# A transformer block in one core: combinations of half blocks, output pops and low halves given out in another order in the feed-forward stage

## The chip, the cores and the metric

The kernel runs on one core of a Trainium2 chip. Times are device microseconds (us) of one execution; the kernel before took 1749.36 us (median of three runs, 1748.49 to 1750.36). The engines are called PE (TensorE, matmuls), DVE (VectorE), ACT (ScalarE), POOL (GpSimd) and SP (SyncE, which issues nearly all DMAs). Each works through its own queue strictly in order, and waits where an operand or a buffer is not ready.

## What is computed

```
mod = (silu(c) @ w_mod) in six parts: sa, ca, ga, sb, cb, gb
h = layernorm(x) * (1 + ca) + sa
x = x + ga * attention(h)                      # 32 heads, 512 keys, wq, wo, cached k and v
h = layernorm(x) * (1 + cb) + sb
x = x + gb * ((gelu(h @ w_gate) * (h @ w_up)) @ w_down)
```

x has 2048 rows of 512 columns, and the feed-forward width F is 1792. All is given and returned in float32.

## The kernel before

**Precision by halves.** Every operand of a large matmul is kept as two float16 tiles, a high half (the rounded value) and a low half (the rest). A product is three matmuls (`mm3`, line 90): low times high, high times high, high times low. The third one is the one that needs the low half of the moving operand. A high half is made by ACT with a copy, a low half by DVE or POOL with a subtraction that reads the high half, so a low half always comes after ACT.

**Seven products for eight.** The projections are computed by a Strassen-like scheme (the Winograd form): a product of 2 x 2 blocks takes seven block products instead of eight, of sums and differences of blocks. `PROD` names the seven products; the feed-forward stage takes them in the order `ORDER = (1, 2, 6, 7, 5, 4, 3)`. Products accumulate in three PSUM banks `fa`, `fb`, `fc`. After products 1, 6 and 7 ACT copies the bank `fa` out (`keep`, line 887) before the next product goes on in it; the results 11, 22, 21 and 12 are made by DVE additions to those copies (line 1272).

**The rows.** The 2048 rows are two halves of 1024. For the second half ("second rows", generation 3) the moving operands of the seven products are the blocks b11, b21, b22 and the combinations t1 to t4. `combos` makes them, in two pairs p=0 and p=1 (two of the four 128-column tiles each): four loads of 256 KB from device memory into raw buffers (`cb`, a pool of five), then seven high halves on ACT (line 374), four differences on POOL (line 576) and seven low halves on POOL (line 378). Each piece has an offset, 0 to 8, which says in what order the pieces come.

**The feed-forward stage** is written out without a scheduler: what Python calls is what the queues get, in that order. It runs over quarters q = 0 to 27. Quarter q belongs to the pair of F tiles n = q // 2 (14 pairs, seven for each half of the rows); even quarters compute the gate (gelu on ACT), odd ones the up product, multiplied on DVE with the gate (line 1288). A quarter has seven places k = 0 to 6, one per product. `step(s, fn)` puts a piece of work at quarter s // 7, place s % 7. At each place these come in order: the product with what follows on it, the pieces of `step`, the work that was put off until now (`put_off(n, fn)` with `tick`), then possibly one pop.

**Activations.** In the odd quarter of pair n the four results are multiplied and split into high half (ACT, line 1298) and low half (line 1302). For n % 7 < 5 the pair is "turned": its down projection uses the seven products too, so behind result 12, the last of the quarter, POOL makes four sums of the results (`sums_of`, line 1314), ACT their high halves and POOL their low halves t1 to t4 (line 1302 on POOL), spread over the next quarter by `put_off`. The other pairs (n = 5, 6, 12, 13) make no sums.

**The down projection** of a turned pair is `yt_tasks(n)`: 14 products in two runs of seven (p = 0, 1), in banks `ya`, `yb`, `yc`, handed out two at a time ("a pop") by `y_next()`. The 14 tasks of pair n enter the list at place k=2 of quarter 2n+2. A pop comes at the places k = 1, 2, 5 and 6 of each quarter. After each y product DVE adds the bank to the result (`yt_add`, lines 1679 and 1682), and the next y product on that bank must wait for it. The first pop has products 1 and 2, the second 6 and 5: product 6 takes t2 and product 5 takes t1. With the last turned pair of a half (n = 4, 11), ACT also makes eight copies of the results (`yu`, line 1698) which SP transposes with DMAs, and POOL adds them to the rows.

**Queue of SP.** Weight sets for quarter q + 1 are fetched from device memory at places k = 2, 3, 4 of quarter q; the loads of the combinations stand in the same queue.

**Where the combinations stand before.** Pair p=0 has its loads at step 59 and its offsets at steps 61, 63, 65 ... 77, pair p=1 at step 73 and 75, 77 ... 91 (`q = 61 + 14 * p`, `step(q + 2 * off, fn)`, lines 1649 to 1654). The results 12 of n=3 and n=4, with which the sums begin, come at steps 55 and 69.

Of the kernel before, what the change touches and what calls it, by code (L numbers as in the profile page):

```python
# [64 lines left out]
def block_kernel(ctx: ExitStack, tc: tile.TileContext, x, kT, v, wq, wo, wg, wu, wd, cT, wc, wm, out):  # L65
    nc = tc.nc
# [7 lines left out]
    def tmp(name):  # L74
        return pool.tile([P, 512], F32, tag="e", name=name, bufs=NE)
# [4 lines left out]
    def pair(tag, name, bufs):  # L80
        return pool.tile([P, 2, 512], F16, tag=tag, name=name, bufs=bufs)
# [96 lines left out]
    def col(name, i=0):  # L178
        return ST[name][:, i:i + 1]
# [113 lines left out]
    def turned(n):  # L293

        return n % NP < NP - NROW
# [160 lines left out]
    def put_off(n, fn):  # L456

        if n == 0:
            return fn()
        waits_.append([n, fn])  # L460
# [219 lines left out]
    def k_items(pr):  # L680
        g = pr // 2
        st, load = reader(kT[g])
        m = {}

        def stat():
            m["m"] = little("lm", 4, dtype=BF16)
            sumsq(m["m"][:, 0:1], st["r"])

        def spread(go=True, ps=None):
            return k_spread(g, m["m"], go, ps)  # L690

        def parts(first=False):
            KV[0, pr, 0] = t = get_k()
            if first:
                return split_post(t, st["r"], col("ksc", pr))
            times(st["r"], col("ksc", pr))
            halves(t, st["r"])

        return (load, stat, spread, parts) + ((m,) if pr == 0 else ())

    def v_items(g):
        st, load = reader(v[g])
        m = {}

        def stat():
            m["m"] = little("lm", 4, dtype=BF16)
            sumsq(m["m"][:, 0:1], st["r"])

        def spread():
            w = little("lw", 1, 2)  # L710
            norm2(col("vmax", g), m["m"], 1, 1.0)
            pool_ts(w, col("vmax", g), 1.0 / TOP14)
            if g:
                y_scale(g)
            then(lambda: nc.vector.reciprocal(col("vsc", g), w), 3 if g > 1 else 2)

        def parts():
            KV[0, g, 1] = get_v()
            times(st["r"], col("vsc", g))
            halves(KV[0, g, 1], st["r"])  # L720

        return load, stat, spread, parts
# [162 lines left out]
    def keep(st, k, t):  # L885
        st[k] = t
        nc.scalar.activation(t, st["a"], AF.Copy)  # L887

    def kept(k):
        return pool.tile([P, QB], F32, tag=k, name=k, bufs=1)  # L890
# [117 lines left out]
    def low(t):  # L1008
        p16 = E[t]["p16"]
        nc.vector.scalar_tensor_tensor(p16[:, 1, :], E[t]["e"], E[t]["r"], p16[:, 0, :], op0=ALU.mult, op1=ALU.subtract)  # L1010
        u, i = divmod(t, 4)
        if i == 0:
            pT[u] = pool.tile([P, QT, 2 * KT, P], F16, tag="pt", name="pt", bufs=NPT)
        nc.sync.dma_start_transpose(pT[u][:, i], p16.rearrange("p a b -> p (a b)"))
        E.pop(t)
# [196 lines left out]
    for g in range(NG):  # L1212
# [24 lines left out]
        else:  # L1237
            if g > 0:
                if pr % 2 == 0:
                    load, stat, spread_, parts = k_items(pr)  # L1240
                    sched(t0 - (22 if g > 2 else 20), (load, [stat]))
                    at(("w", t0 - (19 if g > 2 else 17)), spread_)
                load, stat, spread_, parts = k_items(pr)
                sched(t0 - (7 if g > 2 else 8 if g > 1 else 6), (load, [parts if g != 2 else lambda parts=parts: soon(parts(True))]))
                at(t0 - (3 if g > 2 else 1 if g > 1 else 2), lambda pr=pr: store(("k", pr), KV[0, pr, 0]))
                if pr % 2 == 0:
                    load, stat, spread_, parts = v_items(qd)
# [7 lines left out]
    NQ = 4 * NP  # L1255
# [7 lines left out]
    def f_scale(q):  # L1263
        return (q // 2) % NP * 2 + q % 2

    def f_items(q, hold=None):
        n, m = divmod(q, 2)
        st = {}
        done = set()

        def add(k, src):
            nc.vector.tensor_tensor(st[k], st[k], st[src], op=ALU.add)

        def gelu(key, src):

            def apply():
                dst = tmp("fg") if key == "21" else src
                nc.scalar.activation(dst, src, AF.Gelu_apprx_tanh, scale=col("finv", f_scale(q)))
                G[n, key] = dst

            return (apply,)

        def result(key, src):
            if m == 0:
                put_off(2 if key == "11" else 0, gelu(key, src)[0])
            else:
                g = G[n, key]
                nc.vector.scalar_tensor_tensor(g, g, col("gsc", n % NP), src, op0=ALU.mult, op1=ALU.mult)  # L1288
                if not turned(n):
                    parts(key, G.pop((n, key)))  # L1290
                elif key != "12":
                    parts(key, g)
                else:
                    sums_of()

        def high_of(key, g):
            t = A[n, key] = pair("ot", "at", NOT)
            nc.scalar.activation(t[:, 0, :], g, AF.Copy)  # L1298

        def low_of(key, g, eng):  # L1300
            t = A[n, key]
            eng.tensor_tensor(t[:, 1, :], g, t[:, 0, :], op=ALU.subtract)  # L1302

        def parts(key, g):
            high_of(key, g)
            if key == "21":
                st["low"] = lambda: low_of(key, g, nc.vector)
            else:
                put_off(3 if key == "11" else 2, lambda: low_of(key, g, nc.vector))

        def sums_of():
            g = {k: G.pop((n, k)) for k in ("11", "12", "21", "22")}
            for o, a, b in (("11", "12", "11"), ("12", "22", "12"), ("22", "22", "11"), ("21", "21", "22")):
                nc.gpsimd.tensor_tensor(g[o], g[a], g[b], op=ALU.subtract)  # L1314
            late = 0 if n else 2
            for key, o, high, low in (("t1", "11", 2, 5), ("t3", "12", 3, 6), ("t2", "22", 4, 5), ("t4", "21", 5, 6)):
                put_off(high + (late if high < 5 else late // 2), lambda key=key, o=o: high_of(key, g[o]))
                put_off(low + late // 2, lambda key=key, o=o: low_of(key, g[o], nc.gpsimd))

        def out_(key, src):  # L1320
            if not hold:
                result(key, src)
            else:
                hold.append(gelu(key, src))

        def place(k):
            if m == 0:
                return pool.tile([P, QB], F32, tag="k", name="fg", bufs=2) if k == "u2" and n else tmp("fg")
            return pool.tile([P, QB], F32, tag="p16", name="fu", bufs=NP16) if k == "s1" else kept(k)

        def after(k):
            done.add(k)
            if k in (1, 6, 7):
                name = {1: "s1", 6: "u2", 7: "u3"}[k]
                keep(st, name, place(name))
            if k == 2:
                add("s1", "b")
                out_("11", st["s1"])
            elif k == 4:
                out_("21", st["a"])  # L1340
            elif k == 3:
                if "low" in st:
                    st["low"]()
                add("u2", "c")
                out_("12", st["u2"])
            if k in (5, 7) and {5, 7} <= done:
                add("u3", "c")
                out_("22", st["u3"])

        tags = {"a": ("s", "fa", 2) if q else ("qa", "fa", 1), "b": ("acc", "fb", NACC), "c": ("acc", "fc", NACC)}  # L1350
        return with_posts(("f", q), 2 + q // (2 * NP), banks(st, tags), after)

    def f_spread_at(q):
# [284 lines left out]
    def step(q, fn):  # L1638
        f_at(q // 7, q % 7, fn)

    for i, q in enumerate((16, 19, 22, 26, 30, 33, 36, 40)):
        load, norm, split, turn = ln_turned(i)
# [3 lines left out]
        step(q + 4, turn)  # L1646
    for q, (qb, dt) in zip((37, 41, 44, 47, 50, 51, 54, 55), ((0, 0), (0, 2), (0, 1), (0, 3), (1, 0), (1, 2), (1, 1), (1, 3))):
        step(q, lambda qb=qb, dt=dt: turned_out(qb, dt))
    for p in range(2):
        q = 61 + 14 * p  # L1650
        for load, steps in combos(3, p, nc.gpsimd):
            step(q - 2, load)
            for off, fn in steps:
                step(q + 2 * off, fn)

    def whole(ti):
        if ti in halfway and ti in joined:
# [100 lines left out]
    for q in range(NQ):  # L1758
        n, m = divmod(q, 2)
        its = items(NG + q) if q < 2 else f_items(q)  # L1760
        for k, pk in enumerate(ORDER):
            if (q, pk) not in f_done:
                all_of(its[pk])
            run(("f", q, k))
            tick()
            if n and k == 2 and m == 0 and turned(n - 1):
                nexty += yt_tasks(n - 1)
            if k in ((1, 2, 5, 6) if q < NQ - 1 else (2, 5)):
                y_next()
        if m == 1 and not turned(n):  # L1770
            for qi, (a, b) in enumerate((("11", "21"), ("12", "22"))):
                for i in range(QT):
                    nexty.append(y_tasks((2 * (n // NP) + qi) * QT + i, [lambda n=n, a=a: A[n, a], lambda n=n, b=b: A[n, b]],
                                         [("f", n, 0), ("f", n, 1)], col("dysc", n % NP), f_final))
# [40 lines left out]
```

## Time and profile before

| what | value |
|---|---|
| median of three runs | 1749.36 us (1748.49 to 1750.36) |
| the profiled execution, whole | 1748.16 us |
| its span on the core | 1745.9 us |
| PE, DVE, ACT, POOL busy | 98%, 82%, 71%, 61% |
| mean granted PE clock | 0.998 |
| feed-forward stage | from about 1355 us to the end |

How to read it: the span is the profiled execution from its first to its last instruction, and the time of a run has some 2.3 us around that. A row of the timeline gives start, duration, engine, line, operation, tile written and tiles read, and the number of equal instructions merged; in brackets the idle time of the engine before it and whose result ended that. A row of the windows gives, after the length, the busy time and the number of instructions of PE, PE's weight loads, DVE, ACT and POOL, then the granted PE clock, the busy share of the DMA engines and GB/s. Matmuls overlap, so the duration of a row with six of them is longer than the distance to the next row.

### The profile page before, as it was taken

Reading aid. Unit: us, or ns where it says so; the run is one execution under the profiler, and the core shown is the slowest. Engines: PE = TensorE matmul, PEld = TensorE weight load, DVE = VectorE, ACT = ScalarE, POOL = GpSimd, SP = SyncE. Lnnn points to the kernel's source line nnn. Section 1 sums busy time; section 2 is a strip of 40 time slices with the busy share of each in tenths; the row PEclk is TensorE's granted clock in tenths of the full one; section 3 lists DMA queues with packets and bytes.
Section 4 is the critical chain, followed back from the end, with each engine's and each line's share of the span. In section 5 each row is a group of like instructions: output and inputs, shape, how many; then the busy total and the mean of one; then the engine's idle time right before and its main releaser. Section 6 shows DMA issues by size and latency. Waiting matters only on the chain.

```text
span 1745.9 us, 26253 instructions
## 1 busy us (share of the span) xinstructions
PE 1716.3 (98%) x8022; PEld 787.6 (45%) x8022; DVE 1423.4 (82%) x2462; ACT 1243.0 (71%) x2797; POOL 1056.9 (61%) x1274
## 2 busy tenths in 40 slices
PE   7999999999999999999999999999999999999998
PEld 5444444444444444444444444444444444344444
DVE  7898898888889899888888888888986787566666
ACT  6988788888879777887777777787774455433442
POOL 4889778776788884655575675654521335643424
PEclk9999999999999999999999999999999999999999
DMA  7999999999999999999999999999986564733353
GB/s 232 220 205 212 211 216 207 222 208 217 215 219 230 208 204 185 212 208 232 202 215 231 213 215 211 205 228 213 196 184 145 153 175 151 191 126 113 95 154 104
DMA packets 690636, 339.82 MB, mean 195 GB/s; under 512 B 578880, under 2 KB 601408, under 8 KB 690496
## 3 DMA queue, kind: packets, MB, share of 16 engines
q1 hardware_dynamic: 690208, 337.63, 85.9%
q8 instruction: 63, 1.03, 0.2%
q14 instruction: 77, 0.63, 0.1%
q10 hardware_dynamic: 288, 0.52, 0.1%
HBM read 135.66 MB, written 61.87 MB: 113 GB/s over the span
## 4 chain that ended last, share of the span: by engine, by line
PE 85%; DVE 5%; ACT 4%; POOL 2%; DMA 2%; issue 1%; SPq 0%; POOLq 0%; DVEq 0%; ACTq 0%
PE py L90 19%; PE po L90 17%; PE ps L90 17%; PE qa L90 8%; PE fa L90 7%; PE qc L90 4%; PE fc L90 4%; PE ya L90 2%; PE qb L90 2%; PE fb L90 2%; DMA pt<-p 1%; PE yc L90 1%; ACT ee L993 1%; ACT p L1005 1%; PE pq L90 1%
## 5 line engine op out<-in xcount | busy, mean ns | idle before, releaser
L993 ACT ACTIVATE ee<-ps,nm 128x512 f32<-128x512 f32 x512 | 350.1, 684 | 189.8 <-DVE nm L984 187.7
L1010 DVE SCALAR_TENSOR_TENSOR p<-ee,rr,p 128x512 f16<-128x512 f32 x512 | 459.9, 898 | 4.5 <-ACT p L1005 4.1
L984 DVE TENSOR_REDUCE nm<-ps 128x1 f32<-128x512 f32 x512 | 350.6, 685 | 106.9 <-PE ps L90 103.7
L90 PE MATMUL ps<-k,qt 128*128 128x512 f16 x1536 | 414.9, 379 | 5.2 <-ACT ee L993 4.1
L1005 ACT ACTIVATE p<-ee,rr 128x512 f16<-128x512 f32 x512 | 364.5, 712 | 20.9 <-DMA pt<-p 10.5
L90 PE MATMUL po<-pt,v 128*128 128x512 f16 x1536 | 373.0, 379 | 2.6 <-DMA pt<-p 2.6
L90 PE MATMUL py<-wo,ot 128*128 128x512 f16 x1536 | 371.5, 379 | 0.0
L90 PEld LDWEIGHTS <-w 128*128 128x128 f16 x2184 | 213.7, 98 | 261.8 <-issue 5.8
L90 PEld LDWEIGHTS <-v 128*128 128x128 f16 x1536 | 149.9, 98 | 184.9 <-DMA pt<-p 2.4
L90 PEld LDWEIGHTS <-ot 128*128 128x128 f16 x1536 | 150.2, 98 | 181.6 <-DVE ot L742 0.5
L90 PEld LDWEIGHTS <-qt 128*128 128x128 f16 x1536 | 145.9, 98 | 176.6 <-issue 4.4
L1314 POOL TENSOR_TENSOR fg<-fg 128x512 f32<-128x512 f32 x40 | 52.6, 1315 | 163.9 <-DVE fg L1288 161.5
L742 DVE SCALAR_TENSOR_TENSOR ot<-po,ot 128x512 f16<-128x512 f32 x128 | 87.8, 686 | 36.7 <-ACT ot L741 36.3
L1298 ACT ACTIVATE at<-fg 128x512 f16<-128x512 f32 x86 | 53.9, 627 | 88.8 <-DVE fg L1288 75.0
L993 ACT ACTIVATION_READ_ACCUMULATOR ee<-ps,nm 128x1 f32 x512 | 100.0, 195 | 0.0
L954 DVE SCALAR_TENSOR_TENSOR acc<-py,ysc,acc 128x512 f32<-128x512 f32 x128 | 94.7, 740 | 5.3 <-PE py L90 5.3
L235 POOL TENSOR_TENSOR lw<-lw,half__86 128x1 f32<-128x1 f32 x37 | 23.3, 631 | 105.2 <-DVE lw L185 105.1
L90 PE MATMUL qa<-t,w 128*128 128x512 f16 x348 | 84.9, 379 | 0.0
L90 PE MATMUL fa<-t,w 128*128 128x512 f16 x336 | 81.6, 379 | 1.3 <-ACT fg L887 0.8
L397 POOL TENSOR_TENSOR rs<-rs,nhalf 128x1 f32<-128x1 f32 x32 | 18.7, 585 | 102.0 <-DVE rs L391 99.1
L741 ACT ACTIVATE ot<-po 128x512 f16<-128x512 f32 x128 | 73.9, 577 | 5.0 <-PE po L90 5.0
L90 PE MATMUL ya<-at,wo 128*128 128x512 f16 x240 | 63.9, 380 | 6.6 <-POOL at L1302 5.7
(241 smaller groups left out, 2763.9 us busy)
## 6 DMA issues: line engine op xcount, KB each, us to landing
w<-kept SPq DMA_DIRECT2D x123, 256.0 KB, 3.3
wo<-kept SPq DMA_DIRECT2D x70, 256.0 KB, 3.2
kept<-stage SPq DMA_DIRECT2D x61, 256.0 KB, 3.3
raw<-in_wo SPq DMA_DIRECT2D x56, 256.0 KB, 3.3
kept<-w SPq DMA_DIRECT2D x39, 256.0 KB, 3.4
rw<-in_wq SPq DMA_DIRECT2D x38, 256.0 KB, 3.1
hs<-hf SPq DMA_DIRECT2D x32, 256.0 KB, 2.8
pt<-p SPq DMA_TRANSPOSE x512, 3.5
```

Source lines behind the costliest of these rows:

```text
L90: nc.tensor.matmul(ps, a, b, start=first and n == 0, stop=last and n == 2, skip_group_check=chain)
L235: nc.gpsimd.tensor_tensor(out, out, half_, op=ALU.pow)
L397: nc.gpsimd.tensor_tensor(st["rs"], st["rs"], nhalf, op=ALU.pow)
L741: nc.scalar.activation(t[:, 0, :], src, AF.Copy, scale=scale)
L742: return lambda: nc.vector.scalar_tensor_tensor(t[:, 1, :], src, scale, t[:, 0, :], op0=ALU.mult, op1=ALU.subtract)
L954: nc.vector.scalar_tensor_tensor(acc[ti], st["p"], by, acc[ti], op0=ALU.mult, op1=ALU.add)
L984: nc.vector.tensor_reduce(nm, E[t]["ps"], axis=AX.X, op=ALU.max, negate=True)
L993: nc.scalar.activation(e, E[t]["ps"], AF.Exp, bias=E[t]["nm"], scale=1.0, accum_out=sm[:, t % 2:t % 2 + 1])
L1005: nc.scalar.activation(p16[:, 0, :], E[t]["e"], AF.Copy, scale=E[t]["r"])
L1010: nc.vector.scalar_tensor_tensor(p16[:, 1, :], E[t]["e"], E[t]["r"], p16[:, 0, :], op0=ALU.mult, op1=ALU.subtract)
L1298: nc.scalar.activation(t[:, 0, :], g, AF.Copy)
L1314: nc.gpsimd.tensor_tensor(g[o], g[a], g[b], op=ALU.subtract)
```

## The change

Three places of the feed-forward stage change.

1. **Combinations.** The pieces of pair p=0 are given out at steps 61, 62, 62, 63, 64, 65, 66, 67, 68 for the offsets 0 to 8, its loads at step 59 as before. Pair p=1 has its loads at step 70 (before 73) and its pieces at 75, 76, 76, 77, 78, 79, 80, 81, 82.
2. **Pops.** In quarter 2, the first with pops, they come at k = 2 and k = 6; before the list allowed k = 1, 2, 5 and 6, and at k = 1 there was nothing to pop. All other quarters are as before (the last one keeps 2 and 5).
3. **Low halves.** In the odd quarters the low half of result 22 is no longer put off by two places but made together with that of result 21, at product 3, directly ahead of the DVE addition there. That is behind the y additions of the pop at k = 5, where before it was ahead of them.

No instruction is added or taken away.

```diff
         def parts(key, g):
             high_of(key, g)
-            if key == "21":
-                st["low"] = lambda: low_of(key, g, nc.vector)
+            if key in ("22", "21"):
+                st.setdefault("low", []).append(lambda: low_of(key, g, nc.vector))
             else:
                 put_off(3 if key == "11" else 2, lambda: low_of(key, g, nc.vector))
...
             elif k == 3:
-                if "low" in st:
-                    st["low"]()
+                for low in st.get("low", ()):
+                    low()
                 add("u2", "c")
                 out_("12", st["u2"])
...
-    for p in range(2):
-        q = 61 + 14 * p
+    for p, (q, at_) in enumerate(((59, (61, 62, 62, 63, 64, 65, 66, 67, 68)), (70, (75, 76, 76, 77, 78, 79, 80, 81, 82)))):
         for load, steps in combos(3, p, nc.gpsimd):
-            step(q - 2, load)
+            step(q, load)
             for off, fn in steps:
-                step(q + 2 * off, fn)
+                step(at_[off], fn)
...
-            if k in ((1, 2, 5, 6) if q < NQ - 1 else (2, 5)):
+            if k in {2: (2, 6), NQ - 1: (2, 5)}.get(q, (1, 2, 5, 6)):
                 y_next()
```

## The prediction

> **What bounds the kernel now.** I read the page first: span and engine shares.
>
> ```profile
> span 1745.9 us, 26253 instructions
> PE 1716.3 (98%) x8022; PEld 787.6 (45%) x8022; DVE 1423.4 (82%) x2462; ACT 1243.0 (71%) x2797; POOL 1056.9 (61%) x1274
> ```
>
> PE is busy for all but 29.6 us, so an edit that leaves the matmuls alone can win only from that remainder. The view of who waited for whom says where PE stood in the feed-forward stage (from 1,355 us on):
>
> ```profile
> PE ya L90 <- POOL at L1302: 5.7, 2, 5.1
> ```
>
> That is two waits on low halves made by POOL, one of 5.1 us. The timeline of PE has the long one, in the steps that the diff reorders (quarter 10, k=5 and k=6):
>
> ```profile
> 1481.00 1.46 PE L90 MATMUL fa<-t,x 128*128 128x512 f16 x6
> 1482.30 0.59 PE L90 MATMUL ya<-at,wo 128*128 128x512 f16 x2
> 1487.98 0.59 PE L90 MATMUL ya<-at,wo 128*128 128x512 f16 x1 [5.09 <-POOL at L1302]
> ...
> 1492.07 0.81 PE L90 MATMUL ya<-at,wo 128*128 128x512 f16 x3
> ```
>
> Columns: start, duration, work. A group of six matmuls takes 1.30 us from start to start (1481.00 to 1482.30), 0.216 each; a pop of two y products is also six. The third `ya` matmul, which needs the low half of t2 of F pair n=4, was due two starts after 1482.30, at 1482.73, and came at 1487.98: 5.25 late. The ten matmuls behind it took 4.09 us (to 1492.07) instead of 2.16: 1.93 more. So the stall costs 7.18 us. The windows confirm it:
>
> ```profile
> 1473.16:1507.84 34.68, 29.58 (x127) 12.77 (x126) 18.68 (x28) 18.13 (x28) 25.20 (x21) 0.90 0.59 144
> ...
> 1592.55:1619.99 27.44, 27.43 (x128) 12.31 (x126) 18.54 (x28) 10.40 (x17) 9.56 (x8) 1.00 0.34 101
> ...
> 1488.00:1492.00 4.00, 4.00 (x10) 1.41 (x10) 1.50 (x2) 0.00 (x0) 4.00 (x4) 0.51 0.03 12
> ```
>
> The same work (two quarters, seven pops) takes 34.68 us here and 27.44 in an undisturbed pair. The granted clock (third column from the end) is 0.51 behind the stall: the ten matmuls ran at half rate. [...]
>
> **Edit A: combinations in consecutive steps.** Why POOL was late:
>
> ```profile
> 1474.59 5.33 POOL L1314 TENSOR_TENSOR fg<-fg 128x512 f32<-128x512 f32 x4 [10.32 <-DVE fg L1288]
> 1479.88 1.26 POOL L576 TENSOR_TENSOR cb<-cb 128x512 f32<-128x512 f32 x1
> ...
> 1484.57 1.15 POOL L378 TENSOR_TENSOR t<-cb,t 128x512 f16<-128x512 f32 x1
> 1485.68 4.47 POOL L1302 TENSOR_TENSOR at<-fg,at 128x512 f16<-128x512 f32 x4
> ```
>
> POOL did the four activation sums of n=4, then five instructions of the first combination pair (1479.88 to 1485.68, 5.8 us), then the four low halves; the second low half, that of t2, ends 4.47/2 after 1485.68, at 1487.9, which is when PE goes on. In the order of the changed program all eleven POOL instructions of this pair stand ahead of the four sums, and the low halves follow the sums directly. Then t2's low ends at 1479.88 + 2.23 = 1482.1, 0.6 us before it is due. The stall goes whole if the eleven are done by 1474.59. Are they?
>
> ```profile
> 1457.54 1.16 POOL L378 TENSOR_TENSOR b<-cb,b 128x512 f16<-128x512 f32 x1 [0.27 <-ACT b L374]
> ...
> 1469.59 0.63 ACT L1298 ACTIVATE at<-fg 128x512 f16<-128x512 f32 x1 [2.28 <-DVE fg L1288]
> ```
>
> and, by tile and line (shortest, median and longest duration in ns):
>
> ```profile
> L374 ACT ACTIVATE t<-cb x28: 612/617/631, 75.8 to 1519.5; 128x512 f16<-128x512 f32 x28
> ...
> L378 POOL TENSOR_TENSOR t<-cb,t x25: 1145/1157/1698, 94.6 to 1523.4; 128x512 f16<-128x512 f32 x25
> ...
> L576 POOL TENSOR_TENSOR cb<-cb x27: 1256/1272/1727, 100.0 to 1512.0; 128x512 f32<-128x512 f32 x27
> ```
>
> The first starts at 1457.54 as now. Seven lows at 1.16 and four differences at 1.27 are 13.2 us, so 1470.7 without waits. The last low waits for ACT's t4 high half, which in the new order stands right behind the high half at 1469.59: 1469.59 + 0.63 + 0.62 + 1.16 = 1472.0. The sums find POOL free with 2.6 us to spare. This wait (POOL behind ACT's t highs) is new at this place; behind it on POOL queue the sums, and for those PE. Gain: **7.18 us**. The second pair moves to 1485 to 1500, behind the low halves of n=4; no POOL work with a deadline for PE stands behind it until the sums of n=7, because n=5 and n=6 form no sums.
>
> What it costs is on ACT: the second pair's high halves now stand among the copies of quarter 11.
>
> ```profile
> 1497.80 0.63 ACT L1298 ACTIVATE at<-fg 128x512 f16<-128x512 f32 x1 [0.88 <-DVE fg L1288]
> 1498.33 1.04 ACT L1698 ACTIVATE yu<-yt 128x1024 uint16<-128x1024 uint16 x1
> 1499.28 0.58 ACT L887 ACTIVATE u<-fa 128x512 f32<-128x512 f32 x1
> ...
> 1499.91 1.46 PE L90 MATMUL fa<-t,w 128*128 128x512 f16 x6
> ```
>
> The new order puts t1's high between the first two rows. It takes a slot of 0.53 (1497.80 to 1498.33), so the copy of bank fa (1499.28, done 1499.86) comes 0.5 later, and PE, which takes bank fa again at 1499.91 right behind it, too. **Cost 0.5 us.** The other highs lie before copies that have a whole product of 1.30 us on another bank ahead of their reader, and the first pair has no `yu` copies beside it; I cost these at nothing, and at 0.5 each (up to three) if that cover is gone.
>
> **Edit B: the first pair's pops.** In quarter 2 the second pop goes from k=5 to k=6, behind product 3.
>
> ```profile
> 1368.20 1.46 PE L90 MATMUL fa<-t,x 128*128 128x512 f16 x6
> 1370.48 0.59 PE L90 MATMUL ya<-at,wo 128*128 128x512 f16 x2 [0.83 <-ACT at L1298]
> 1371.72 0.38 PE L90 MATMUL ya<-at,wo 128*128 128x512 f16 x1 [0.64 <-POOL at L1302]
> ...
> 1370.51 3.38 POOL L1302 TENSOR_TENSOR at<-fg,at 128x512 f16<-128x512 f32 x3 [0.90 <-ACT at L1298]
> ```
>
> Now `ya` was due at 1368.20 + 1.30 = 1369.50 and came 0.98 late; its third matmul, due 0.43 behind 1370.48, came at 1371.72, 0.81 late: 1.79 us. Behind product 3 the pop is due at 1370.80, when ACT's half is there; its third matmul at 1371.23 still waits for POOL's low (ready 1371.72, POOL's order there is unchanged): 0.49 stay. **Gain 1.30 us.** It lies between 0 (POOL's lows come later by as much) and 1.79. All later pops of n=0 shift by one place and the last goes to a free place in quarter 4: the same matmuls.
>
> **Edit C: low halves behind additions.** In each odd quarter with pops, DVE makes the low half of result 22 ahead of two y additions:
>
> ```profile
> 1386.67 0.69 DVE L1302 TENSOR_TENSOR at<-fg,at 128x512 f16<-128x512 f32 x1
> 1387.28 0.75 DVE L1682 TENSOR_SCALAR yt<-ya,dyc 128x512 f32<-128x512 f32 x1
> 1388.13 0.75 DVE L1679 SCALAR_TENSOR_TENSOR yt<-yc,dyc,yt 128x512 f32<-128x512 f32 x1
> ...
> 1388.12 0.81 PE L90 MATMUL ya<-at,wo 128*128 128x512 f16 x3
> 1388.93 0.81 PE L90 MATMUL yc<-at,wo 128*128 128x512 f16 x3
> ...
> 1700.82 0.81 PE L90 MATMUL ya<-at,wo 128*128 128x512 f16 x3
> 1701.64 0.81 PE L90 MATMUL yc<-at,wo 128*128 128x512 f16 x3
> ```
>
> `yc` goes on in a bank that the addition must have read. Three matmuls take 0.65; here 0.81 pass: PE waits 0.16 until the addition ends at 1388.88. The gap stands in the ten odd quarters of n=0 to 4 and 7 to 11 (first and last shown). With the low half behind the additions these end 0.6 us sooner; the low half still runs before the next addition on DVE, so what follows is not later. **Gain 10 x 0.16 = 1.6 us**; between 0, if something else ends the gap, and 1.6.
>
> **Sum.** 7.18 + 1.30 + 1.6 - 0.5 = 9.6 us. The profiled execution took 1748.16 us (span 1745.9 and 2.3 around it) and would take 1738.6; the median of the three timed runs, 1749.36, is 1.2 above it, so I forecast **1739.8 us**.
>
> **Rivals.**
>
> 1. **POOL is stretched.** The eleven instructions now run without pauses beside DVE. Were each as long as the longest of its kind (1.70 and 1.73, rows above), that is 0.54 x 7 + 0.46 x 4 = 5.6 us more: done at 1476.3 instead of 1470.7, the sums 1.7 us late, and PE, with 0.6 of slack, 1.1 late. If the last low also waits for a late t4 high, about 2.5. Time 1741 to 1742.5. For it: the long ones exist. [...] Against: medians sit at the short end, and POOL's slack takes most. Chance 0.18.
>
> 2. **The stall is not where the change looks for it**: another producer is just as late, as ACT's half was at 1370.48, and only edits B and C count: 1749.36 - 2.9 + 0.5 = 1747.0, within 0.2%. Against: the row of 1487.98 names POOL, whose second low half ends then. Chance 0.06.
>
> 3. **SyncE's queue blocks (slower).** The second pair's four loads move from step 73 to 70, ahead of all weight fetches of quarter 11. Today:
>
> ```profile
> 1472.26 19.35 SPq L96 DMA_DIRECT2D cb<-hs  x4
> ...
> w<-kept SPq DMA_DIRECT2D x19, 256.0 KB, 3.9
> ```
>
> The loads hold the queue until the first pair's third raw buffer is free, at 1491.6. Were it free no sooner in the new order, quarter 11's first weights would land 3.9 us later, at 1495.5, for matmuls due at 1486.2 (now one group behind 1492.07, at 1493.37, less 7.18): 9.3 us idle and 1.93 at half rate, 11.2 lost against 9.6 won: 1751.0, slower. From a release after 1482.3 on PE waits; from about 1490 on the change loses. Against: that buffer is released by t2's low, which moves ahead of the sums, before 1472. Chance 0.04, half of it beyond 0.2%.
>
> **How the numbers follow.** Forecast 0.72 (own range 1737.5 to 1741.5: the 0.49 and the 0.5 gone or doubled, edit C at half, a run's scatter of 1), rivals 0.18, 0.06, 0.04. The range of 1737.0 to 1744.0 takes in forecast and rival 1, and leaves out rivals 2 and 3. A measurement of this kernel can tell about 0.2%, 3.5 us, from no change. Faster by more: 0.9 (forecast and rival 1); within: 0.08 (rival 2 and half of 3); slower: 0.02.
>
> **What would show it.** Right: the wait of `ya` on POOL shrinks to one of about 0.5 near 1371; no stretch at a granted clock near 0.5 in quarter 10; POOL's four sums and four lows of n=4 adjacent; first pair's last low before 1474; y additions ahead of two adjacent low halves, and `yc` 0.65 behind `ya`. Wrong: a wait of `ya` on POOL over 1 us in quarter 10 (rival 1), PE waiting for DMA at the start of quarter 11 (rival 3), or a new wait of `fa` on ACT copies in quarter 11 much above 0.5.

## The result, and the profile after

The changed kernel took **1740.12 us** (median of four runs, 1739.80 to 1740.85) beside 1748.92 us (1748.28 to 1750.36) of the kernel before on the same chip: ratio 0.9949, 95% interval 0.9932 to 0.9966. It is faster by 0.3 to 0.7%. 1739.8 was forecast. The profiled execution took 1740.01 us. Its page:

```profile
span 1737.8 us, 26247 instructions
...
PE 1712.5 (99%) x8020; PEld 786.6 (45%) x8022; DVE 1426.1 (82%) x2462; ACT 1242.4 (71%) x2797; POOL 1056.9 (61%) x1274
```

The span is 8.1 shorter, and the busy times of DVE, ACT and POOL stand within 3 us of those before: work was moved, not removed. Who PE waited for, after (engine, tile, whom; us in total, times, longest):

```profile
PE fa L90 <- ACT fg L887: 0.9, 3, 0.3
PE fa L90 <- ACT u L887: 0.9, 2, 0.5
PE ya L90 <- DVE yt L1678: 0.7, 1, 0.7
PE ya L90 <- POOL at L1302: 0.3, 1, 0.3
```

Before, beside the row on POOL that the prediction shows:

```profile
PE ya L90 <- ACT at L1298: 0.8, 1, 0.8
PE fa L90 <- ACT fg L887: 0.8, 3, 0.3
PE fa L90 <- ACT u L887: 0.4, 1, 0.4
```

The 5.7 us behind POOL have shrunk to 0.3. The waits on ACT come to 1.8 for 2.0 before, partly at other places; the wait on DVE is new. PE's timeline after, at all the places that the prediction spoke of (quarter 2, an odd quarter, quarters 10 and 11):

```profile
1371.51 0.59 PE L90 MATMUL ya<-at,wo 128*128 128x512 f16 x2
1372.44 0.38 PE L90 MATMUL ya<-at,wo 128*128 128x512 f16 x1 [0.34 <-POOL at L1302]
...
1414.74 0.81 PE L90 MATMUL ya<-at,wo 128*128 128x512 f16 x3
1415.39 0.81 PE L90 MATMUL yc<-at,wo 128*128 128x512 f16 x3
...
1477.26 1.46 PE L90 MATMUL fa<-t,w 128*128 128x512 f16 x6 [0.32 <-ACT fg L887]
...
1481.14 0.81 PE L90 MATMUL ya<-at,wo 128*128 128x512 f16 x3
1481.79 0.81 PE L90 MATMUL yc<-at,wo 128*128 128x512 f16 x3
...
1490.21 0.81 PE L90 MATMUL yb<-at,wo 128*128 128x512 f16 x3
1491.70 0.81 PE L90 MATMUL ya<-at,wo 128*128 128x512 f16 x3 [0.68 <-DVE yt L1678]
1492.99 1.46 PE L90 MATMUL fa<-t,w 128*128 128x512 f16 x6 [0.48 <-ACT u L887]
```

In quarter 10 (1481.14) the three `ya` matmuls follow one another, with no stall. In quarter 2 the third one is 0.50 late, as forecast (1372.44 for 1371.94). `yc` follows `ya` after 0.65. New are two waits in quarter 11: `ya` is due at 1490.86 and comes 0.84 late, `fa` is due at 1492.35 and comes 0.64 late; and one in quarter 10, `fa` at 1477.26, 0.47 late. POOL after:

```profile
1469.67 1.16 POOL L378 TENSOR_TENSOR t<-cb,t 128x512 f16<-128x512 f32 x1 [0.24 <-ACT t L374]
1473.44 5.33 POOL L1314 TENSOR_TENSOR fg<-fg 128x512 f32<-128x512 f32 x4 [2.61 <-DVE fg L1288]
1478.73 4.51 POOL L1302 TENSOR_TENSOR at<-fg,at 128x512 f16<-128x512 f32 x4
```

The first pair's last low half ends at 1470.83, POOL sits idle 2.6 us, and sums and low halves stand one behind the other. The windows from quarter 10's first product to quarter 12's, then quarters 10 and 11 alone:

```profile
1471.60:1500.76 29.16, 27.68 (x128) 12.32 (x126) 20.47 (x28) 18.54 (x29) 23.44 (x19) 1.00 0.60 161
1471.60:1485.01 13.41, 13.10 (x61) 5.87 (x60) 8.24 (x13) 7.75 (x13) 11.26 (x10) 1.00 0.45 127
1485.01:1500.76 15.75, 14.58 (x68) 6.45 (x66) 12.22 (x16) 10.79 (x17) 12.19 (x10) 1.00 0.72 189
```

29.16 in place of 34.68, at a granted clock of 1.00.

**How the kernels are compared from here on.** The stage is counted from quarter 2's first product to the end of the span. What comes before it is the same program in every kernel here, yet its length differs between executions (bank `fb` of quarter 2 begins between 1361.7 and 1363.6 us in the fourteen profiles), more than most effects below. The stage leaves that out: **385.47 us before, 376.65 after, 8.82 less.** One thing inside the stage differs between executions too, where PE has stood for 5.1 us: how long the half rate behind that goes on. The matmuls behind the wait lose 1.9 us to it in the profile before, 2.1 in that of B alone and 2.5 in that of C alone, so their quarters 10 differ by up to 0.6 for that reason. The pieces are cut at the first product on `fb` of each quarter (the stage has one product, 1.29, ahead of the first piece). Edit B moves one pop, 1.30, from quarter 2 into quarter 4.

| quarters | before | after | A alone | B alone | C alone | A and B |
|---|---|---|---|---|---|---|
| 2, 3 | 29.15 | 26.40 | 29.15 | 27.01 | 28.99 | 27.03 |
| 4, 5 | 27.76 | 28.49 | 27.76 | 28.65 | 27.63 | 28.66 |
| 6 to 9 | 55.82 | 55.56 | 56.23 | 55.83 | 55.56 | 56.22 |
| 10 | 20.21 | 13.42 | 12.96 | 20.40 | 20.87 | 12.97 |
| 11 | 14.48 | 15.73 | 15.95 | 14.48 | 14.31 | 15.96 |
| 12, 13 | 28.85 | 28.49 | 28.49 | 28.85 | 29.08 | 28.62 |
| 14, 15 | 28.49 | 28.49 | 28.49 | 28.49 | 29.48 | 28.49 |
| 16 to 26 | 151.35 | 150.67 | 151.34 | 151.35 | 150.68 | 151.37 |
| 27 to end | 28.07 | 28.10 | 28.09 | 28.00 | 28.20 | 28.11 |
| stage | 385.47 | 376.65 | 379.75 | 384.35 | 386.09 | 378.72 |

### The profile page after: what moved, and what is told of

Read it like the earlier page. It is cut to its first block, busy times and chain, and to the rows that moved or that the text cites. A ratio compares the mean times of both kernels' runs of the same rounds, so it can differ in the third digit from the quotient of the medians.

```text
span 1737.8 us, 26247 instructions
## 1 busy us (share of the span) xinstructions
PE 1712.5 (99%) x8020; PEld 786.6 (45%) x8022; DVE 1426.1 (82%) x2462; ACT 1242.4 (71%) x2797; POOL 1056.9 (61%) x1274
## 4 chain that ended last, share of the span: by engine, by line
PE 86%; DVE 5%; ACT 4%; POOL 2%; DMA 2%; issue 1%; SPq 0%; DVEq 0%; POOLq 0%; ACTq 0%
PE py L90 20%; PE po L90 17%; PE ps L90 17%; PE qa L90 8%; PE fa L90 7%; PE qc L90 4%; PE fc L90 4%; PE ya L90 2%; PE qb L90 2%; PE fb L90 2%; DMA pt<-p 1%; PE yc L90 1%; ACT p L1005 1%; ACT ee L993 1%; PE pq L90 1%
## 5 line engine op out<-in xcount | busy, mean ns | idle before, releaser
L159 POOL TENSOR_TENSOR stage<-rw,stage 128x512 f16<-128x512 f32 (+1 forms) x56 | 64.4, 1150 | 4.7
```

Of the source, the lines that this page charges most:

```text
L159: nc.gpsimd.tensor_tensor(dst[:, 1, :], src, dst[:, 0, :], op=ALU.subtract)
```

## The experiments

**Theory**: edit A removes the stall, with B and C worth their gaps beside it. **Rivals**: the gain comes from another edit, or the second pair of combinations rather than the first; and a term of the sum is no loss or gain of its own but hangs on another edit.

### Each edit alone

A alone: the kernel before with only the steps of the combinations changed.

```diff
-    for p in range(2):
-        q = 61 + 14 * p
+    for p, (q, at_) in enumerate(((59, (61, 62, 62, 63, 64, 65, 66, 67, 68)), (70, (75, 76, 76, 77, 78, 79, 80, 81, 82)))):
...
-                step(q + 2 * off, fn)
+                step(at_[off], fn)
```

> Edit A alone (both combination pairs in consecutive steps), on the kernel before. The stage is counted from the first fa product of quarter 2 to the end of the span: 385.5 us before, 376.7 in the changed kernel. Theory (each edit removes a wait of its own, and A's is the late low half of t2): the 5.1 us wait of ya on POOL and the half rate behind it go, 7.2 us, less 1.5 of new waits in quarter 11, so a stage of 379.8 and a time some 5.7 us under the kernel before. The yc gaps of 0.16 and the 1.8 us in quarter 2 stay. Rival (the edits work only together): under 2 us.

Measured: 1742.93 us, ratio 0.9968 [0.9956, 0.9980]; stage 379.75, that is 5.72 less than before. Quarter 10 falls by 7.25, quarters 9 and 11 rise by 0.41 and 1.47.

B alone: the kernel before with only the pops of quarter 2 changed.

```diff
-            if k in ((1, 2, 5, 6) if q < NQ - 1 else (2, 5)):
+            if k in {2: (2, 6), NQ - 1: (2, 5)}.get(q, (1, 2, 5, 6)):
```

> Edit B alone (pops of quarter 2 at k=2 and 6), on the kernel before. Theory: 1.45 us in quarters 2 and 3, and 0.4 more in quarter 4, where the pop at k=1 now stands between product 2 and product 6 and gives ACT time for its copy: stage 383.6, time 1.9 us under before, which is less than the runs can tell alone, but the windows can. The 5.1 us wait stays. Rival (the low half of t2 comes later by as much): stage 385.4.

Measured: 1748.14 us, ratio 0.9994 [0.9984, 1.0003]; stage 384.35, 1.12 less. The stall of quarter 10 stays. Quarters 2 and 3 gain 0.84 (with the moved pop) and not 1.30, since a new wait takes 0.46 of it (PE's timeline of this kernel):

```profile
1387.66 0.81 PE L90 MATMUL ya<-at,wo 128*128 128x512 f16 x3 [0.46 <-DVE yt L1682]
```

C alone: the kernel before with only the low half of result 22 moved.

```diff
-            if key == "21":
-                st["low"] = lambda: low_of(key, g, nc.vector)
+            if key in ("22", "21"):
+                st.setdefault("low", []).append(lambda: low_of(key, g, nc.vector))
...
-                if "low" in st:
-                    st["low"]()
+                for low in st.get("low", ()):
+                    low()
```

> Edit C alone (low half of 22 behind the y additions), on the kernel before. Theory: the ten gaps of 0.16 us ahead of yc close, stage 383.9, 1.6 us under before. The 5.1 us wait stays. Rival (something else ends those gaps, or result 12 comes later by the two low halves in a row): stage 385.5 or more, with yc still 0.81 behind ya.

Measured: 1748.86 us, ratio 1.0000 [0.9990, 1.0009]; stage 386.09, 0.62 **more**. That was not expected. The gaps of `yc` do close (quarters 16 to 26: 0.67 less), but quarter 14 loses 0.99 and quarter 10 0.66. Of the 0.66 only 0.04 is a longer wait (of `fa` on ACT's copy); the rest is the half rate behind the stall, which goes on longer in this execution (the same window before, then with C alone; granted clock 0.67 and 0.56):

```profile
1488.00:1494.00 6.00, 6.00 (x19) 2.29 (x19) 3.16 (x5) 0.72 (x1) 5.92 (x6) 0.67 0.25 56
...
1488.00:1494.00 6.00, 5.94 (x16) 2.16 (x16) 2.58 (x4) 0.69 (x1) 5.92 (x7) 0.56 0.24 52
```

The loss in quarter 14 is a wait of its own. PE, DVE and POOL of this kernel around the start of quarter 14, one view each:

```profile
1542.32 1.46 PE L90 MATMUL fa<-t,w 128*128 128x512 f16 x6 [0.82 <-ACT fg L887]
```

```profile
1535.55 0.74 DVE L954 SCALAR_TENSOR_TENSOR acc<-py,dysc,acc 128x512 f32<-128x512 f32 x1
1536.21 3.23 DVE L1302 TENSOR_TENSOR at<-fg,at 128x512 f16<-128x512 f32 x2
```

```profile
1535.95 4.62 POOL L1658 TENSOR_TENSOR acc<-acc,yr 128x512 f32<-128x512 f32 x3
```

The two low halves in a row on DVE (3.23), of quarter 13's results, stand beside POOL's additions to the rows; elsewhere, with POOL idle, the pair takes 1.28. Result 12 of that quarter waits behind them on DVE, the copy of bank `fa` behind result 12 on ACT, and PE behind the copy.

What follows: alone the three are worth -5.72, -1.12 and +0.62, in sum -6.22; together they are worth -8.82. So 2.60 us of the gain belong to no edit by itself. Of these, 0.85 is only the longer half rate in the profiles of B alone (0.19) and C alone (0.66), which is gone where A is in. The rest is a wait that one edit makes and another clears: 1.0 in quarter 14 and 0.2 in quarter 12 (made by C, cleared by A), 0.45 in quarter 3 (made by B, cleared by C).

### Which pair of combinations

The changed kernel with the second pair at the old, wide steps.

```diff
-(70, (75, 76, 76, 77, 78, 79, 80, 81, 82))
+(73, (75, 77, 79, 81, 83, 85, 87, 89, 91))
```

> The changed kernel with the second pair as before: loads at step 73, pieces every second step from 75 to 91. Theory (the first pair ahead of the sums is the whole of A's gain, and the dense second pair costs 1.5 us in quarter 11 and gives 0.4 back in quarter 12): no wait of ya over 0.5 us, stage 375.5, 1.1 us under the changed kernel. Rival (the gain came from the earlier loads, which let SP's queue go on): the wait of ya on POOL is back and the stage is 382 to 384.

Measured: 1740.72 us, ratio 0.9953 [0.9938, 0.9968]; stage 377.96. No stall of `ya` on POOL comes back, and quarter 11 falls to 14.31, as expected. The stage is not the 375.5 expected, though: quarter 14 shows the loss of C alone again (quarters 14 and 15 take 29.47, `fa` 0.82 idle behind ACT's copy), and 8 to 10 lose 1.2.

The changed kernel with the first pair at the old steps.

```diff
-(59, (61, 62, 62, 63, 64, 65, 66, 67, 68))
+(59, (61, 63, 65, 67, 69, 71, 73, 75, 77))
```

> The changed kernel with the first pair as before (pieces every second step from 61 to 77), the second dense and loaded at step 70. Theory (POOL's order decides, and the third rival's mechanism is real where the first pair is late): the wait of ya on POOL is back with 5.2 us and 1.9 at half rate, and the loads hold SP's queue, so that quarter 11's first weights come 2 us or more late for PE: stage 385 to 387, no faster than before. Rival (the earlier loads are what helps): stage under 380.

Measured: 1749.60 us, ratio 1.0004 [0.9994, 1.0014]; stage 385.44, quarter 10 23.31. PE's timeline and its window behind the stall:

```profile
1485.85 0.58 PE L90 MATMUL ya<-at,wo 128*128 128x512 f16 x1 [5.09 <-POOL at L1302]
...
1494.29 1.47 PE L90 MATMUL fa<-b,w 128*128 128x512 f16 x6 [3.28 <-DMA w<-kept]
```

```profile
1485.85:1490.00 4.15, 4.15 (x13) 1.54 (x13) 1.68 (x3) 0.00 (x0) 4.15 (x4) 0.62 0.03 11
```

So the **first** pair holds the gain of A. The second row is the mechanism of rival 3: the second pair's loads block SP's queue until the first pair frees its raw buffers, and quarter 11's weights come late. SP in this kernel (the four loads end at 1489.49, and the weights are issued behind them):

```profile
1460.78 28.71 SPq L96 DMA_DIRECT2D cb<-hs  x4
```

The changed kernel with the second pair four steps later from its second piece on.

```diff
-(70, (75, 76, 76, 77, 78, 79, 80, 81, 82))
+(70, (79, 80, 80, 81, 82, 83, 84, 85, 86))
```

> The changed kernel with the second pair four steps later, at 79 to 86, equally dense. In the changed kernel the DVE product of result 11 in quarter 11 took 1.72 us instead of 0.75 while POOL did differences, and ya waited for the addition behind it. Theory (it is POOL beside DVE): with POOL idle there that product takes 0.75, the wait of ya on DVE goes (0.8 us), and fa's wait for the u copy falls from 0.6 to 0.1; a new wait of up to 0.5 on ACT copies in quarter 12: stage 375.4 to 376. Rival (the DVE instruction is slow for another reason, such as DMAs): 1.7 us again and the same wait, stage 376.7.

Measured: 1741.65 us, ratio 0.9959 [0.9944, 0.9974]; stage 378.21. Quarter 11 falls to 14.40 with both new waits gone, as the theory said; but quarter 12 takes 2.9 us more, which it did not say. DVE and PE of this kernel:

```profile
1487.93 0.75 DVE L1288 SCALAR_TENSOR_TENSOR fg<-fg,gsc,fu 128x512 f32<-128x512 f32 x1
...
1497.97 2.50 DVE L1302 TENSOR_TENSOR at<-fg,at 128x512 f16<-128x512 f32 x2
```

```profile
1504.71 1.46 PE L90 MATMUL fa<-t,w 128*128 128x512 f16 x6 [1.91 <-ACT fg L887]
...
1508.12 1.46 PE L90 MATMUL fa<-t,w 128*128 128x512 f16 x6 [0.66 <-ACT fg L887]
```

With POOL idle the product of result 11 takes 0.75; the pair's work now stands beside the two low halves (2.50) and its t highs ahead of the copies of `fa` in quarter 12.

### How the stall is priced

The changed kernel with two, and with three, of the first pair's last low halves (and their high halves) behind the sums.

```diff
-(59, (61, 62, 62, 63, 64, 65, 66, 67, 68))
+(59, (61, 62, 62, 63, 64, 65, 66, 69, 70))
```

```diff
-(59, (61, 62, 62, 63, 64, 65, 66, 67, 68))
+(59, (61, 62, 62, 63, 64, 65, 69, 70, 71))
```

> The changed kernel with the last two pieces of the first pair one step and two steps later (69 and 70), so that two low halves of 1.15 us stand on POOL between the four sums and the low halves of n=4. Theory: t2's low half comes 2.3 us later, 0.6 of that is slack: ya waits 1.7 us, stage 378.4. The wait is shorter than the 5.25 us behind which the clock fell, and I expect no half rate behind it; if there is one, the stage is 380.3.

Measured: 1742.74 us, ratio 0.9963 [0.9950, 0.9976]; stage 379.13. The third `ya` was due at 1482.18 (0.43 behind 1481.75) and came 1.70 late:

```profile
1481.75 0.59 PE L90 MATMUL ya<-at,wo 128*128 128x512 f16 x2
1483.88 0.38 PE L90 MATMUL ya<-at,wo 128*128 128x512 f16 x1 [1.54 <-POOL at L1302]
```

> As the run before with three low halves behind the sums (last pieces at 69, 70, 71). Theory: t2's low half comes 3.45 us later, ya waits 2.9 us, stage 379.6 without a half rate behind it, 381.5 with one. With the run before and the changed kernel it gives a line: 1.15 us of PE time for each POOL instruction beyond the slack of 0.6.

Measured: 1743.12 us, ratio 0.9965 [0.9954, 0.9977]; stage 379.62. Due at 1483.10, 2.81 late; the window shows the clock (PE's timeline, then the windows):

```profile
1482.67 0.59 PE L90 MATMUL ya<-at,wo 128*128 128x512 f16 x2
1485.91 0.38 PE L90 MATMUL ya<-at,wo 128*128 128x512 f16 x1 [2.65 <-POOL at L1302]
```

```profile
1482.00:1488.00 6.00, 3.35 (x16) 1.46 (x15) 1.76 (x3) 2.21 (x4) 6.00 (x6) 1.00 0.78 231
```

One POOL instruction more ahead of the deadline costs PE one instruction's length (1.11 from two to three; on POOL the low halves behind the sums take 2.24 for two and 3.34 for three, to the start of the next row). The rows of the wait show that; the stages hold more (quarters 8 and 9 take 0.9 and 0.8 more than in the changed kernel, and quarter 11 takes 0.7 less in the second), so it is partly luck that the second stage came out as expected. The clock stays at 1.00 behind 2.65 us of idle time; it had fallen to 0.51 (before) and 0.62 (first pair spread) behind 5.1.

### What C is worth beside A and B

The changed kernel with the low half of result 22 put off by two places again (C's diff above, reversed).

> The changed kernel without edit C (low half of result 22 made two places after its high half again, ahead of the y additions); A and B stay. The stage is counted from quarter 2's first product to the end of the span: 376.65 us in the changed kernel. Theory (C is worth its gaps because the dense second pair keeps POOL clear of the two adjacent low halves): the ten gaps of yc come back, 0.81 instead of 0.65 between ya and yc, less where another wait already covers one, 1.3 to 1.6 us; quarter 2 to 4 becomes 27.0 as with B alone (0.6 more, ya on a DVE addition); quarters 14 to 16 stay at 28.5. Stage 378.6 to 378.9, some 2 us slower than the changed kernel. Rival (C is worth nothing beside A either, as it was worth nothing alone): stage 376.4 to 377.2.

Measured: 1741.53 us, ratio 0.9956 [0.9943, 0.9970]; stage 378.72. C is worth 2.07 here and about nothing alone. Quarters 2 to 5 give 0.80 of it and the later ones, with the gaps of `yc`, 1.72; quarter 10 takes back 0.45: without C, `fa` has no wait there. ACT in quarter 10, without C and then after:

```profile
1477.06 0.58 ACT L887 ACTIVATE fg<-fa 128x512 f32<-128x512 f32 x1
```

```profile
1476.63 0.58 ACT L887 ACTIVATE fg<-fa 128x512 f32<-128x512 f32 x1
```

Quarter 10 began at 1472.49 without C and at 1471.60 after, so the copy comes 4.57 and 5.03 behind that: result 12 is 0.5 later behind the start of the quarter, and so are POOL's sums, ACT's high half of t3 and the copy behind that. The two low halves ahead of result 12 do not do this by themselves: with C alone the copy comes 4.67 behind the start of the quarter, for 4.63 before, and with the first pair at its old steps 4.66. It takes the dense first pair beside them, whose last low halves on POOL meet DVE at the end of quarter 9. DVE there after, then with two of those low halves moved behind the sums (the experiment of two above):

```profile
1467.42 0.99 DVE L1288 SCALAR_TENSOR_TENSOR fg<-fg,gsc,u 128x512 f32<-128x512 f32 x1
...
1470.50 1.47 DVE L1302 TENSOR_TENSOR at<-fg,at 128x512 f16<-128x512 f32 x2
```

```profile
1468.45 0.75 DVE L1288 SCALAR_TENSOR_TENSOR fg<-fg,gsc,u 128x512 f32<-128x512 f32 x1
...
1471.30 1.28 DVE L1302 TENSOR_TENSOR at<-fg,at 128x512 f16<-128x512 f32 x2
```

In the second, with C in place, the copy comes at 4.60 and `fa` has no such wait. Without C the same slowing of DVE costs as much one quarter earlier: quarter 9 takes 0.41 more with A alone than before, in a wait of `ya` on a y addition.

### Is there a better order?

Three orders that take the new waits away. First, the four t high halves of the second pair two steps later:

```diff
-(70, (75, 76, 76, 77, 78, 79, 80, 81, 82))
+(70, (75, 76, 76, 77, 80, 81, 82, 83, 84))
```

> The changed kernel with the four t high halves of the second pair (and what hangs on them) two steps later, at 80 to 84, so that none stands between the high half of result 11 and the copy of bank fa in quarter 11. Theory (edit A's cost on ACT is one slot of 0.53 ahead of that copy): the wait of fa on the u copy in quarter 11 (0.48 idle, 0.64 late) goes; the wait of ya on a DVE addition there (0.84 late) stays if DVE's product of result 11 is the one that is slowed beside POOL. Stage 376.0 (376.65 less 0.64), or 375.2 if by chance POOL is slowed and not DVE. Rival (the copy is late because the product of result 11 is late on DVE, not because of the t high): the wait of fa keeps most of its 0.64; stage 376.5. Against both, as with the second pair at 79 to 86: a pair that ends later stands beside DVE's low halves in quarter 12, and result 12 comes later there: 377 or more.

Measured: 1740.29 us, ratio 0.9950 [0.9936, 0.9963]; stage 377.55. `fa`'s wait in quarter 11 is gone, `ya`'s stays, as the theory had it, but quarter 12 takes 1.3 more, as with the later pair (PE's timeline):

```profile
1504.95 1.46 PE L90 MATMUL fa<-t,w 128*128 128x512 f16 x6 [1.17 <-ACT fg L887]
```

Second, these steps and t3's high half of the sums one place later:

```diff
-("t3", "12", 3, 6), ("t2", "22", 4, 5)
+("t3", "12", 4 if n else 3, 6), ("t2", "22", 4, 5)
```

> As the run before (second pair's t pieces at 80 to 84), and the high half of sum t3 one place later for all pairs but the first, so that in the quarter after a turned pair ACT copies bank fa of product 6 before it makes that half. Theory: the waits of fa on the fg copy in quarters 6, 8 and 10 (about 0.44 late each) and the small ones in the second half of the rows (about 0.1 each) go, t3's low is made no later than now because POOL reaches it behind two others: 1.3 to 1.7 us. Stage 374.3 to 375.2, about 1738. Rival (t3's high held up: the low of t3, t2 or t4 comes later, and ya waits on POOL for what is won): stage as in the run before.

Measured: 1739.66 us (1739.22 to 1739.88), ratio 0.9945 [0.9931, 0.9958]; stage 376.76. The waits in quarter 10 and the second half of the rows go (0.4 each), quarter 6 gets a wait on POOL instead, and quarter 12 keeps its 1.3.

Third, only t1 of the second pair later, and the sums' t3 one place later and behind t2:

```diff
-(70, (75, 76, 76, 77, 78, 79, 80, 81, 82))
+(70, (75, 76, 76, 77, 79, 79, 80, 81, 82))
...
-("t3", "12", 3, 6), ("t2", "22", 4, 5)
+("t2", "22", 4, 5), ("t3", "12", 4 if n else 3, 6)
```

> The changed kernel (stage 376.65 us) with only the t1 high half of the second pair one step later (79 in place of 78, behind the copy of bank fa; t3 to t4 stay at 79 to 82), and for all pairs but the first the high half of sum t3 one place later and behind that of t2, so that in the quarter after a turned pair ACT copies bank fa of product 6 first and t2 is not held up. Theory: fa's wait on the u copy in quarter 11 goes (0.5 to 0.6); the waits of fa on the fg copy in quarters 6, 8 and 10 go without a wait of ya on POOL in their place (0.4 each), and 0.45 in the second half of the rows; the t4 high stays ahead of quarter 12, which keeps its 14.25. 376.65 - 0.55 - 1.2 - 0.45: stage 374.3 to 375.0, about 1738. Rival (POOL, one slot later with t1 and its successors, still stands beside the two low halves of DVE in quarter 11, as with the pair two steps later): quarter 12 becomes longer by 0.5 to 1.3, stage 375 to 376.

Measured: 1740.28 us, ratio 0.9950 [0.9936, 0.9963]; stage 377.50. The rival was right on quarter 12 (15.56 for 14.25), the waits of `fa` moved on to the next product (1480.42, 0.48 idle), and DVE's product of result 11 was slowed in quarter 9. None of the three can be told from the changed kernel; no version faster than it was found.

## Why the prediction was right

The time came out 0.3 us from the forecast, but the terms were not all right; some errors cancel, and that it is as near as 0.3 is luck (see the total).

- **Edit A, 7.18**: right in size (7.25 with A alone) and in cause. Its two steps, that PE is late by the POOL instructions ahead of t2's low and that the half rate follows, are separate: two and three instructions (PE 1.70 and 2.81 late) gave the first without the second. The second, 1.93 in the profile before, is 2.1 with B alone, 2.5 with C alone, and 1.5 with the first pair at its old steps, where the ten matmuls took 3.70 for 2.16 (1485.85 to 1489.55).
- **A's cost, 0.5**: too small: 1.4 in quarter 11 (15.73 against 14.31 to 14.40 where the second pair is elsewhere) and 0.4 more in quarter 10. The slot of 0.53 on ACT that was priced is right (with the t highs moved, quarter 11 takes 0.52 less). The step that failed is that it was the only one: the cost was looked for on ACT alone, and nothing in the sum stood for DVE being slowed beside POOL, beside the first pair at the end of quarter 9 (0.99 and 1.47 for 0.75 and 1.28, rows above) and beside the second in quarter 11. DVE after, in quarter 11, and POOL beside it:

```profile
1488.61 1.72 DVE L1288 SCALAR_TENSOR_TENSOR fg<-fg,gsc,fu 128x512 f32<-128x512 f32 x1
1490.25 1.40 DVE L1678 SCALAR_TENSOR_TENSOR yt<-ya,dyc,yt 128x512 f32<-128x512 f32 x2
```

```profile
1487.16 2.62 POOL L576 TENSOR_TENSOR cb<-cb 128x512 f32<-128x512 f32 x2
1489.74 1.61 POOL L378 TENSOR_TENSOR b<-cb,b 128x512 f16<-128x512 f32 x1
```

  The product of result 11 took 1.72 in place of 0.81 before; the y additions queue behind it, and `ya` waits for them. Rival 1 had POOL's instructions longer beside DVE, and not DVE's beside POOL.
- **Edit B, 1.30**: right (1.45 with C's gap of 0.16 in the same quarter), with the 0.49 left as said. Alone it gives 0.84 there: C was needed to remove the wait on a y addition. Another 0.41 in quarter 4 was not foreseen; it comes with B, alone too (27.35 less the moved pop, for 27.76). Why is argued only: the pop in front gives ACT time for the copy that `fa` waits for there.
- **Edit C, 1.6**: the ten gaps closed. The step "the low half still runs before the next addition on DVE, so what follows is not later" holds to 0.04 where POOL is idle: six copies of `fa`, in quarters 6, 8, 18, 20, 22 and 24, make PE wait that much longer. Beside POOL it fails: by 0.5 in quarter 10, where the dense first pair does it, and with C alone by a whole microsecond in quarter 14, beside POOL's additions to the rows, which is more than the gaps in quarters 16 to 26 are worth (0.67). That quarter 14 is not lost in the changed kernel is owed to A: the dense second pair lets POOL go through its eight additions earlier, so that six are done when the low halves of quarter 13 come, and only four with C alone. With the second pair spread the loss is back.
- **Not in the sum**: quarter 12 gains 0.36, since the second pair's t highs no longer stand ahead of ACT's copies of `fa` there.
- **The total**: 9.6 forecast, 8.82 measured in the stage. A's cost (0.9 more in quarter 11, 0.4 in quarter 10) against quarters 4 and 12 (0.41 and 0.36) leaves 0.5 less than forecast, and the six copies of `fa` take another 0.25. The profiled execution was 1.4 over its forecast of 1738.6; the other 0.7 of that lies ahead of the stage (its first product at 1361.15 for 1360.43), in a part that no edit touches. The median was forecast by adding 1.2, its distance from the profiled execution before; after, that distance is 0.1. So an error of 1.4 and one of 1.1 nearly cancel. That the 1.2 before comes from the half rate of varying length is likely but not shown.
- **Rival 1** (POOL stretched): some of the first pair's instructions were stretched (two differences in quarter 9 took 3.04 for 2.62), but POOL still had the 2.6 us to spare that the sum gave it, since its last low half waited for ACT. **Rival 2** falls with the first pair's experiment. **Rival 3**: the mechanism is real, as the first pair at its old steps showed, but not in the changed kernel: SP's row of the four loads is 8.46 long there and ends at 1469.78, 15 us ahead of quarter 11's first product (1485.03).

```profile
1461.32 8.46 SPq L96 DMA_DIRECT2D cb<-hs  x4
```

## What to carry to other kernels

Where a deadline is missed, count the instructions that the late engine executes between its release and the one that is waited for: each cost its own length here (1.11 us), and moving them ahead of the release, into the engine's idle time, won it all (7.25 us of quarter 10). But each place that such a block moves to has another engine's work beside it: price that engine's instructions at their disturbed duration (1.72 us for 0.75 here), not only the block's. And test edits of one change together and apart: one that is worth nothing alone can be worth 2 us beside another that clears its place. Where half rate follows a stall, as it did the 5.1 us here, take its price from more than one profile: it was 1.5 to 2.5.

## What the runs showed of the hardware

**DVE and POOL side by side.** In quarters 9 and 11 DVE's product of result 11 meets POOL's two differences in a row. DVE and POOL after, in quarter 9 (quarter 11 stands above):

```profile
1460.94 0.75 DVE L1288 SCALAR_TENSOR_TENSOR fg<-fg,gsc,fu 128x512 f32<-128x512 f32 x1
```

```profile
1459.80 3.04 POOL L576 TENSOR_TENSOR cb<-cb 128x512 f32<-128x512 f32 x2
```

In quarter 9 DVE starts 1.14 behind POOL's first difference, takes 0.75 and POOL 3.04. In quarter 11 it starts 1.45 behind, takes 1.72, and POOL 2.62 (1.28 and 1.27, where the median of such a difference is 1.27). In quarter 11 of the kernel before, DVE starts 0.22 ahead of the first difference and takes 0.81, and POOL takes 3.08. Over all runs with these two side by side, starts of 1.10 to 1.28 behind went as in quarter 9, those from 1.34 on as in quarter 11, and starts at 1.30 and 1.31 went either way (one at 0.81 slowed DVE a little, to 1.00). POOL's second difference begins 1.35 behind the first in quarter 9 after (at 1461.15, 0.21 behind DVE's start; it takes 1.68) and 1.36 behind it in quarter 11 (at 1488.52, 0.09 ahead of DVE's; it takes 1.27). So in these runs it fits the outcome, to some hundredths, to ask which of the two starts first: the other is the one that is slowed. Why it goes by that, no view shows. A few hundredths of a microsecond decide over 0.8 us of PE's time here (`ya` 0.84 late in quarter 11), and quarters 8 and 9 together cost 0.8 to 1.1 more in four of the experiments (both ways of leaving low halves behind the sums, the second pair spread, and the third of the other orders).

**The clock.** PE idle for 5.1 us was followed by a granted clock of 0.51 or 0.62, idle for 2.65 by one of 1.00. But 2.65 is not a length that these runs show to be safe: before, PE's last matmul ahead of the wait ended at 1482.89, and the granted clock was 1.00 from 1484.9 to 1485.0 and 0.50 from 1485.1 to 1485.2, so the fall came only 2.2 us behind that matmul; with C alone (1482.96) the clock from 1484 to 1488 was 0.80 on average, which, with one fall from 1.00 to 0.50, puts it at about 1486.4, 3.4 behind. Between one execution and the other the fall thus moved by 1.2 us; what sets it is not shown.
